# Attention weights turned in quarters of the array: 32 products of 64x64 in place of eight full transposes

## The chip, the core and the metric

The kernel runs on one core of one Trainium2 chip. The metric is the device time of one execution in microseconds. Work on a core is shared among TensorE (PE, matmuls, written to PSUM), VectorE (DVE), ScalarE (ACT), GpSimd (POOL, unused here but for set-up) and the DMA queues (SP issues them).

## What is computed

Attention within chunks of 64 tokens, and behind it a channel mix with a shift by one token. All tensors are FP32; 8 batches, 8 heads, 576 tokens, head size 64, so 512 channels; the inner width of the mix is 1024.

```python
scores = scale * np.matmul(q_c, k_c.transpose(0, 1, 2, 4, 3))   # chunks of 64 tokens
scores = scores - np.max(scores, axis=-1, keepdims=True)
attn = np.exp(scores)
attn = attn / (np.sum(attn, axis=-1, keepdims=True) + 1e-09)
x = np.matmul(attn, v_c)                                        # back to [batch, token, channel]
xk = mu_k * x + (1.0 - mu_k) * x_prev                           # x_prev: the token before
xr = mu_r * x + (1.0 - mu_r) * x_prev
k = np.maximum(xk @ w_k, 0.0)
out = 1.0 / (1.0 + np.exp(-(xr @ w_r))) * (k * k @ w_v)
```

## The kernel before

The 4608 tokens are cut into 18 groups of 256, each two tiles (`tl`) of 128 tokens, each of these two chunks of 64 (`e`). Groups 0 to 2 are done in an opening whose steps stand in a list of their own (`START`). From group 2 on `group(g)` records the steps of a group under names, and the table `GROUP` sets by hand in which order they are issued; no scheduler changes it (`manual_schedule`). While group g goes through the mix, the attention of group g + 1 is done between its products. `group_attention` is called with g + 1 for 15 groups, 3 to 17; these are the regular groups that the change touches.

Attention of a group runs like this. `group_products` (`s`, L973) multiplies queries and keys: 32 products of 64x64 by 64 columns, each in one quarter of the array. The rows of the array that a product uses follow from the partitions of its operands, the columns from the partitions of its output. VectorE and ScalarE make the weights `pg` of it: `[token in chunk pair, tl, head, 64 keys]`, 128 partitions. The weights must then be turned, so that keys lie on partitions. That is `f_tr` (step `Pq.0`): eight transposes of 128x128, one for each tile and pair of heads (`hp`), go to `pt` in PSUM, two banks. `f_pT` (`Pq.1`, ScalarE) copies `pt` to `pTg`. `f_pv` (`Pq.2`) multiplies by the values into `xps` (L1058), again 32 products of 64x64 by 64 columns in quarters.

On TensorE the transposes stand between the last `pk` product (`moe_k`, L593, the first product of the mix) and the first `pr` product (`moe_r`, L647, 24 of them). Behind `pr` come `xps`, the scores `s` of the group after, and the products `vx` and `vyz` (L870) of the mix. `pk`, `pr`, `vx` and `vyz` use the whole array, with operands in F32R; attention and its transposes are in F32. In the opening, `move_qk` (`trk` and `trq`, L357) turns queries and keys by plain matmuls with `ident`, 64 columns of the array at a time:

```python
for hp in range(HP):
    for j in range(2):
        nc.tensor.matmul(
            x[halves[j], hp, :],
            T[f"{nm}{g}"][:, j * HP + hp, r, :],
            ident,
```

Of the kernel before, what the change touches and what calls it, by code (L numbers as in the profile page):

```python
# [7 lines left out]
F32 = mybir.dt.float32  # L8
# [3 lines left out]
AF = mybir.ActivationFunctionType  # L12
# [4 lines left out]
P = 128  # L17
CH = 64
TT = 128
# [60 lines left out]
def tile_chunk_attention_channel_mix(  # L80
# [12 lines left out]
    nc = tc.nc  # L93
# [3 lines left out]
    HP = H // 2  # L97
# [23 lines left out]
    ps_s = ctx.enter_context(tc.tile_pool(name="ps_s", bufs=1, space=PSUM))  # L121
# [5 lines left out]
    T = {}  # L127
# [5 lines left out]
    ident = const.tile([P, P], F32, name="ident")  # L133
# [128 lines left out]
    def quarter(h, c):  # L262

        n = 10 * (h + 1) + c + 1
        if n not in B:
            B[n] = wts.tile([P, 2, HF, HD], F32R, tag=f"b{n}", name=f"b{n}")
        return B[n]
# [77 lines left out]
    halves = [slice(j * CH, (j + 1) * CH) for j in range(2)]  # L345
# [99 lines left out]
    def x_tile(g):  # L445
        return xp.tile([P, NB, G + 4], F32, tag="x", name=f"x_{g}")

    def x_cuts(t):

        cut = -t * TT % S  # L450
        if 0 < cut < TT:
            return [(0, cut, 0), (cut, TT - cut, cut + 1)]
        return [(0, TT, 0)]
# [533 lines left out]
    def group_attention(g):  # L987
        do.task = f"S{g}c"

        def heads(x):  # L990
            return x.rearrange("p t h c -> p (t h) c")

        def scores():
            return T[f"s{g}"].rearrange("p j t h c -> p j (t h) c")

        def p():
            return heads(T[f"pg{g}"])

        def f_max(_):
            m = T[f"m{g}"] = par_m.tile([P, 2, H], F32, tag="m", name=f"m_{g}", bufs=1)  # L1000
            nc.vector.tensor_reduce(out=m, in_=scores(), axis=AX.X, op=ALU.max)

        def f_sub(_):
            T[f"pg{g}"] = att.tile([P, 2, H, CH], F32, tag="p", name=f"p_{g}", bufs=1)
            m = T[f"m{g}"].unsqueeze(3).to_broadcast([P, 2, H, CH])
            to = T[f"pg{g}"].rearrange("p t (h j) c -> p j (t h) c", j=2)
            nc.vector.tensor_tensor(to, scores(), m, ALU.subtract)

        def f_exp(_):
            nc.scalar.activation(p(), p(), AF.Exp, scale=1.0 / D**0.5)  # L1010

        def f_z(_):
            T[f"z{g}"] = par_z.tile([P, 2 * H], F32, tag="z", name=f"z_{g}", bufs=1)
            nc.vector.tensor_reduce(out=T[f"z{g}"], in_=p(), axis=AX.X, op=ALU.add)

        def f_eps(_):
            nc.vector.tensor_scalar_add(T[f"z{g}"], T[f"z{g}"], 1e-9)

        def f_inv(_):
            nc.vector.reciprocal(T[f"z{g}"], T[f"z{g}"])  # L1020

        def f_norm(_):
            z = T[f"z{g}"].unsqueeze(2).to_broadcast([P, 2 * H, CH])
            nc.vector.tensor_tensor(p(), p(), z, ALU.mult)

        do(f_max, "D")
        do(f_sub, "D")
        do(f_exp, "A")
        do(f_z, "D")
        do(f_eps, "D")  # L1030
        do(f_inv, "D")
        do(f_norm, "D")

        do.task = f"P{g}q"

        def f_tr(_):
            T[f"pt{g}"] = ps_s.tile([P, 2, HP, TT], F32, tag="s", name=f"pt_{g}")
            for tl in range(2):
                for hp in range(HP):
                    nc.tensor.transpose(  # L1040
                        out=T[f"pt{g}"][:, tl, hp, :],
                        in_=T[f"pg{g}"][:, tl, 2 * hp : 2 * hp + 2, :],
                        identity=ident,
                    )

        def f_pT(_):
            T[f"pTg{g}"] = att.tile([P, 2, HP, TT], F32, tag="p", name=f"pT_{g}", bufs=1)
            nc.scalar.activation(T[f"pTg{g}"], T[f"pt{g}"], AF.Copy)

        def f_pv(_):  # L1050
            T[f"xps{g}"] = ps_x.tile([P, NB, G], F32, tag="x", name=f"xps_{g}")
            for tl in range(2):
                for a in range(HP // 2):
                    for e in range(2):
                        for c in range(2):
                            for j in range(2):
                                hp = 2 * a + c
                                nc.tensor.matmul(  # L1058
                                    T[f"xps{g}"][
                                        halves[c], 2 * j + a, tl * TT + e * CH : tl * TT + (e + 1) * CH  # L1060
                                    ],
                                    T[f"v{2 * g + tl}"][halves[j], hp, e, :],
                                    T[f"pTg{g}"][halves[j], tl, hp, halves[e]],
                                    start=True,
                                    stop=True,
                                )

        def f_open(_):
            x = T[f"xg{g}"] = x_tile(g)
            if g * G % S == 0:  # L1070
                nc.vector.memset(x[:, :, 0:1], 0.0)
            elif g == 3:
                seg = x_cuts(2 * g - 1)[-1]
                last = seg[2] + seg[1]
                nc.vector.tensor_copy(out=x[:, :, 0:1], in_=xt[2 * g - 1][:, :, last : last + 1])
            else:
                s, n, c = group_cuts(g - 1)[-1]
                nc.vector.tensor_copy(out=x[:, :, 0:1], in_=T[f"xg{g - 1}"][:, :, c + n : c + n + 1])
            for s, n, c in group_cuts(g)[1:]:
                nc.vector.memset(x[:, :, c : c + 1], 0.0)  # L1080

        def f_x(_):
            for s, n, c in group_cuts(g):
                nc.scalar.activation(
                    T[f"xg{g}"][:, :, c + 1 : c + 1 + n], T[f"xps{g}"][:, :, s : s + n], AF.Copy
                )

        do(f_tr, "P")
        do(f_pT, "A")
        do(f_pv, "P")  # L1090
        do(f_open, "D")
        do(f_x, "A")

    def group_cuts(g):
        cut = -g * G % S
        if 0 < cut < G:
            return [(0, cut, 0), (cut, G - cut, cut + 1)]
        return [(0, G, 0)]
# [52 lines left out]
    for i in range(4):  # L1151
        h = i // 2
# [5 lines left out]
            lambda s, h=h, part=part: [quarter(h, c)[:, s, part, :] for c in range(2)],  # L1158
            ("kk", "kk", "st", "st")[i],
        )  # L1160
    for t in range(6):
# [5 lines left out]
        if t in (1, 3):  # L1167
            g = t // 2
# [12 lines left out]
    with tc.manual_schedule():  # L1181
        for word in START.split():
            name, _, e = word.partition(":")
# [105 lines left out]
```

## Time and profile before

| | us |
|---|---|
| median of 3 runs | 562.09 |
| lowest and highest of them | 561.68, 562.21 |
| the profiled execution, its own time | 561.84 |
| its span, first to last instruction | 560.1 |
| TensorE busy | 553.5 (99%) |
| VectorE busy | 462.8 (83%) |
| ScalarE busy | 346.1 (62%) |
| matmuls recorded on TensorE | 6432 |

The table is read so: the span is the profiled execution's time less what lies around it (1.7 us here); an engine's busy time is the time in which at least one of its instructions ran. Matmuls overlap in the array, so one of 64 columns is shown with some 218 ns though the next starts long before that is over; their pace is read from starts, not from durations.

### The profile page before, as it was taken

The numbers are of one execution on the slowest core, as the hardware profiler recorded it, in microseconds if no ns is written. First come the engines' busy times: TensorE is split into PE (matmuls) and PEld (weight loads), VectorE is DVE, ScalarE is ACT, GpSimd is POOL, SyncE is SP. The second block draws the span as 40 slices with busy tenths as digits, with TensorE's granted clock in tenths as the row PEclk, the third lists the DMA queues.
The fourth block names the chain that finished last, engine by engine and source line by source line (L and its number), as shares of the span: only waits on it lengthen the run. The fifth ranks groups of instructions, "written<-read, shape, count | busy, mean of one in ns | idle before, by whom it ended". The sixth has DMA issues, their size and how long they took to land.

```text
span 560.1 us, 15245 instructions
## 1 busy us (share of the span) xinstructions
PE 553.5 (99%) x6432; PEld 526.1 (94%) x6432; DVE 462.8 (83%) x789; ACT 346.1 (62%) x509; POOL 0.7 (0%) x6
## 2 busy tenths in 40 slices
PE   9999999999999999999999999999999999999997
PEld 8888999999999999999999999999999999999997
DVE  2999999999897879787888978887888788876834
ACT  5899941739474756657565747483929292938461
POOL 0000000000000000000000000000000000000000
PEclk9999999999999999999999999999999999999999
DMA  9997534444343433421243434343343402010011
GB/s 284 278 285 204 133 76 94 69 69 110 67 107 66 94 69 79 69 72 40 57 67 94 66 89 66 91 71 90 65 99 59 103 1 76 3 45 33 3 38 37
DMA packets 184276, 49.24 MB, mean 88 GB/s; under 512 B 169608, under 2 KB 176272, under 8 KB 184208
## 3 DMA queue, kind: packets, MB, share of 16 engines
q1 hardware_dynamic: 183904, 48.01, 37.9%
q8 instruction: 50, 0.82, 0.7%
q10 hardware_dynamic: 304, 0.27, 0.1%
q14 instruction: 18, 0.15, 0.1%
HBM read 38.80 MB, written 9.44 MB: 86 GB/s over the span
## 4 chain that ended last, share of the span: by engine, by line
PE 90%; ACT 7%; DMA 2%; DVE 0%; issue 0%; ACTq 0%
PE pk L593 33%; PE pr L647 16%; PE vx L870 15%; PE vyz L870 11%; PE pv L681 6%; PE xps L1058 3%; PE s L973 3%; PE pt L1040 2%; DMA k_ring<-in_k 2%; PE warm L1186 1%; ACT wk L141 1%; PE trk L357 1%; ACT wv_st L295 1%; ACT wv_st L299 1%; ACT relu L614 0%; ACT wk_st L299 0%
## 5 line engine op out<-in xcount | busy, mean ns | idle before, releaser
L593 PE MATMUL pk<-xkhi,wk 128*128 128x256 f32 (+1 forms) x1167 | 202.0, 276 | 0.2 <-ACT relu L614 0.2
L593 PEld LDWEIGHTS pk<-xkhi,wk 128*128 128x128 f32 x1167 | 177.1, 188 | 0.7 <-ACT relu L614 0.4
L593 PE MATMUL pk<-xklo,wk 128*128 128x256 f32 x576 | 160.0, 278 | 0.1
L593 PEld LDWEIGHTS pk<-xklo,wk 128*128 128x128 f32 x576 | 108.2, 188 | 0.5 <-DVE xklo L566 0.5
L614 ACT ACTIVATE rr<-pk 128x512 f32<-128x512 f32 x60 | 35.3, 589 | 114.3 <-PE pk L593 114.3
L647 PE MATMUL pr<-wr,xrhi 128*128 128x512 f32 x288 | 90.4, 395 | 0.0
L870 PE MATMUL vx<-b,ks 128*128 128x256 f32 x540 | 68.5, 276 | 0.0
L870 PE MATMUL vyz<-b,kk 128*128 128x256 f32 x540 | 68.5, 276 | 0.0
L870 PEld LDWEIGHTS vyz<-b,kk 128*128 128x128 f32 x540 | 64.5, 188 | 0.0
L870 PEld LDWEIGHTS vx<-b,ks 128*128 128x128 f32 x540 | 64.5, 188 | 0.0
L647 PEld LDWEIGHTS pr<-wr,xrhi 128*128 128x128 f32 x288 | 52.7, 188 | 10.3
L647 PE MATMUL pr<-wr,xrlo 128*128 128x512 f32 x144 | 56.2, 390 | 0.0
L899 ACT ACTIVATE u<-vx 128x256 f32<-128x256 f32 x30 | 11.5, 384 | 54.3 <-PE vx L870 54.3
L708 DVE TENSOR_TENSOR kk<-rr,kk 128x1024 fp32r<-128x1024 f32 x30 | 35.4, 1222 | 10.7 <-ACT kk L854 10.6
L621 ACT ACTIVATE rr<-rr 128x512 f32<-128x512 f32 x60 | 38.0, 633 | 1.9
L708 DVE TENSOR_TENSOR xklo<-mk,xkhi 128x1024 fp32r<-128x1024 f32 x15 | 18.4, 1225 | 25.1 <-ACT xkhi L1130 25.1
L681 PE MATMUL pv<-b,kk 128*128 128x256 f32 (+1 forms) x290 | 34.3, 278 | 0.0
L681 PEld LDWEIGHTS pv<-b,kk 128*128 128x128 f32 x290 | 33.4, 188 | 0.1
L647 PEld LDWEIGHTS pr<-wr,xrlo 128*128 128x128 f32 x144 | 27.0, 188 | 5.7
L708 DVE TENSOR_TENSOR ks<-ss,ks 128x512 fp32r<-128x512 f32 x45 | 28.3, 684 | 0.0
L1120 DVE SCALAR_TENSOR_TENSOR mk<-d,mu,x 128x256 f32<-128x256 f32 (+3 forms) x80 | 27.7, 413 | 0.4
L1120 DVE SCALAR_TENSOR_TENSOR mr<-d,mu,x 128x256 f32<-128x256 f32 (+3 forms) x80 | 27.5, 411 | 0.0
(119 smaller groups left out, 839.4 us busy)
## 6 DMA issues: line engine op xcount, KB each, us to landing
v<-in_v SPq DMA_DIRECT2D x144, 64.0 KB, 2.6
out<-sg SPq DMA_DIRECT2D x34, 256.0 KB, 2.3
q_ring<-in_q SPq DMA_DIRECT2D x192, 36.0 KB, 2.1
k_ring<-in_k SPq DMA_DIRECT2D x192, 36.0 KB, 2.2
wk_st<-in_moe_w_k SPq DMA_DIRECT2D x4, 1024.0 KB, 9.4
wv_st<-in_moe_w_v SPq DMA_DIRECT2D x4, 1024.0 KB, 7.5
wr_st<-in_moe_w_r SPq DMA_DIRECT2D x2, 1024.0 KB, 8.1
k_ring<-in_k SPq DMA_DIRECT2D x2, 512.0 KB, 7.3
```

What stands on the lines that cost most here:

```text
L593: nc.tensor.matmul(pk[:, e, part], wk[a][:, cb, f * P : (f + 1) * P], xk[b][:, cb, part], start=(n == 0 and part is parts[0]), stop=(n == ...
L614: nc.scalar.activation(r, T[f"pk{g}{fp}"], AF.Relu)
L621: nc.scalar.activation(r, r, AF.Square)
L647: nc.tensor.matmul(pr, xr[a][:, cb, tl * TT : (tl + 1) * TT], wr[b][:, cb, :], start=(n == 0), stop=(n == 3 * NB - 1),)
L681: nc.tensor.matmul(T[f"pv{g}{tl}"][:, cols[c]][:, part], kk[a][:, f, tok[tl]], quarter(f // HF, c)[:, b, f % HF, part], start=(f == 0 and ...
L708: nc.vector.tensor_tensor(to, x, y, ALU.subtract)
L870: nc.tensor.matmul(to, a[i][:, f, :], weight(w, j, f), start=first and f == 0 and n == 0, stop=f == HF - 1 and n == 2, skip_group_check=True,)
L899: nc.scalar.activation(T[f"u{g}"][n // 2][:, n % 2], src(), AF.Copy)
L973: nc.tensor.matmul(T[f"s{g}"][halves[e], j, tl, hp, :], qT[halves[j], hp, cols], kT[halves[j], hp, cols], start=True, stop=True,)
L1040: nc.tensor.transpose(out=T[f"pt{g}"][:, tl, hp, :], in_=T[f"pg{g}"][:, tl, 2 * hp : 2 * hp + 2, :], identity=ident,)
L1058: nc.tensor.matmul(T[f"xps{g}"][halves[c], 2 * j + a, tl * TT + e * CH : tl * TT + (e + 1) * CH], T[f"v{2 * g + tl}"][halves[j], hp, e, :] ...
L1120: nc.vector.scalar_tensor_tensor(out=to[:, cb, s : s + w], in0=T[f"d{g}"][:, cb, s : s + w], scalar=mu[:, cb : cb + 1], in1=T[f"xg{g}"][:, ...
```

## The change

In `f_tr` each transpose of 128x128 gives way to four plain matmuls, one for each quarter: the moving operand is a 64x64 block of `ident`, the stationary one a 64x64 block of the weights (chunk `e`, head `2 * hp + j`). That is 32 products for a group. `pt` takes another layout, with `e` outside, so that the products of one half of the array's rows write one bank. `f_pT` copies the same 1024 elements of each partition and puts them in the old order as it writes, in runs of 64. `pTg` and all that reads it stay as they are, and so does the transposing in the opening (`att_values`).

```diff
--- before.py
+++ after.py
@@ -1034,18 +1034,26 @@
         do.task = f"P{g}q"
 
         def f_tr(_):
-            T[f"pt{g}"] = ps_s.tile([P, 2, HP, TT], F32, tag="s", name=f"pt_{g}")
+            T[f"pt{g}"] = ps_s.tile([P, 2, 2, HP, CH], F32, tag="s", name=f"pt_{g}")
             for tl in range(2):
                 for hp in range(HP):
-                    nc.tensor.transpose(
-                        out=T[f"pt{g}"][:, tl, hp, :],
-                        in_=T[f"pg{g}"][:, tl, 2 * hp : 2 * hp + 2, :],
-                        identity=ident,
-                    )
+                    for e in range(2):
+                        for j in range(2):
+                            nc.tensor.matmul(
+                                T[f"pt{g}"][halves[j], e, tl, hp, :],
+                                T[f"pg{g}"][halves[e], tl, 2 * hp + j, :],
+                                ident[halves[e], halves[e]],
+                                start=True,
+                                stop=True,
+                            )
 
         def f_pT(_):
             T[f"pTg{g}"] = att.tile([P, 2, HP, TT], F32, tag="p", name=f"pT_{g}", bufs=1)
-            nc.scalar.activation(T[f"pTg{g}"], T[f"pt{g}"], AF.Copy)
+            nc.scalar.activation(
+                T[f"pTg{g}"].rearrange("p t h (e c) -> p e (t h) c", e=2),
+                T[f"pt{g}"].rearrange("p e t h c -> p e (t h) c"),
+                AF.Copy,
+            )
 
         def f_pv(_):
             T[f"xps{g}"] = ps_x.tile([P, NB, G], F32, tag="x", name=f"xps_{g}")
```

No step changes its place. TensorE's instructions around the turn in one of the regular groups, from the last two `pk` products to the third `pr`, are these before (in a row: line, operation, output and operands, size of the output, count):

```order
L593 MATMUL pk_3_3258<-xklo_3035,wk_118 128x256
L593 MATMUL pk_3_3258<-xkhi_3034,wk_119 128x256
L1040 MATMUL pt_3283<-ident,p_3175 128x128 x8
L647 MATMUL pr_0_3313<-wr_120,xrhi_3180 128x512
L647 MATMUL pr_0_3313<-wr_121,xrhi_3180 128x512
L647 MATMUL pr_0_3313<-wr_120,xrlo_3181 128x512
```

and these with the change:

```order
L593 MATMUL pk_3_3354<-xklo_3131,wk_118 128x256
L593 MATMUL pk_3_3354<-xkhi_3130,wk_119 128x256
L1042 MATMUL pt_3379<-ident,p_3271 64x64 x32
L647 MATMUL pr_0_3433<-wr_120,xrhi_3276 128x512
L647 MATMUL pr_0_3433<-wr_121,xrhi_3276 128x512
L647 MATMUL pr_0_3433<-wr_120,xrlo_3277 128x512
```

Only the row in the middle is another one: 32 matmuls of 64x64 stand where eight of 128x128 stood, behind the same `pk` and ahead of the same `pr`.

## Rows read from the trace of the kernel before

**Rows 1.** The page: busy time, share and instructions; TensorE's granted clock by slices.
```profile
PE 553.5 (99%) x6432; PEld 526.1 (94%) x6432; DVE 462.8 (83%) x789; ACT 346.1 (62%) x509; POOL 0.7 (0%) x6
...
PEclk9999999999999999999999999999999999999999
```

**Rows 2.** The page's chain that ended last, by line.
```profile
PE pk L593 33%; PE pr L647 16%; PE vx L870 15%; PE vyz L870 11%; PE pv L681 6%; PE xps L1058 3%; PE s L973 3%; PE pt L1040 2%; DMA k_ring<-in_k 2%; PE warm L1186 1%; ACT wk L141 1%; PE trk L357 1%; ACT wv_st L295 1%; ACT wv_st L299 1%; ACT relu L614 0%; ACT wk_st L299 0%
```

**Rows 3.** The chain in order of time, a regular group: start us, us, what.
```profile
444.38 11.01 PE pk L593 x97
455.38 0.87 PE pt L1040 x8
456.26 5.47 PE pr L647 x24
461.73 1.09 PE xps L1058 x64
462.82 0.93 PE s L973 x64
463.75 1.57 PE vx L870 x12
465.32 1.36 PE vyz L870 x12
```

**Rows 4.** Line L1040, whole span: records, min/median/max ns; what TensorE waited for.
```profile
L1040 PE MATMUL pt<-ident,p x120: 270/272/273, 104.3 to 514.2; 128*128 128x128 f32 x120
its engine sat idle before it (us, times) until:
```

**Rows 5.** Timeline of TensorE around one `pt`: start us, us, instructions.
```profile
455.10 0.28 PE L593 MATMUL pk<-xkhi,wk 128*128 128x256 f32 x1
455.22 1.03 PE L1040 MATMUL pt<-ident,p 128*128 128x128 f32 x8
...
456.56 0.40 PE L647 MATMUL pr<-wr,xrlo 128*128 128x512 f32 x1
```

**Rows 6.** Timeline of TensorE in the last group.
```profile
541.49 0.28 PE L593 MATMUL pk<-xkhi,wk 128*128 128x256 f32 x1
...
542.07 0.39 PE L647 MATMUL pr<-wr,xrlo 128*128 128x512 f32 x1
```

**Rows 7.** Lines L973 and L357, whole span (x: records; ns).
```profile
L973 PE MATMUL s<-kT,qT x960: 218/218/267, 92.2 to 492.6; 64*64 64x64 f32 x192
...
L357 PE MATMUL trk<-ident,k_ring x96: 272/273/475, 5.3 to 30.6; 128*64 128x128 f32 x96
```

**Rows 8.** Timeline of TensorE from `pr` to `xps` and `s`.
```profile
461.34 0.39 PE L647 MATMUL pr<-wr,xrlo 128*128 128x512 f32 x1
461.66 1.16 PE L1058 MATMUL xps<-pT,v 64*64 64x64 f32 x64
462.64 1.11 PE L973 MATMUL s<-kT,qT 64*64 64x64 f32 x64
```

**Rows 9.** Timeline of TensorE in the opening: products in quarters, then `pr`.
```profile
24.08 0.69 PE L400 MATMUL s<-kT,qT 64*64 64x64 f32 x32
24.59 0.65 PE L484 MATMUL xps<-pT,v 64*64 64x64 f32 x32
...
25.74 0.40 PE L647 MATMUL pr<-wr,xrlo 128*128 128x512 f32 x1
```

**Rows 10.** Timeline of TensorE from `pv` to `s`.
```profile
122.51 0.50 PE L681 MATMUL pv<-b,kk 128*128 128x256 f32 x3
122.94 0.28 PE L973 MATMUL s<-kT,qT 64*64 64x64 f32 x3
```

**Rows 11.** Timelines of VectorE and of ScalarE around the same `pt`.
```profile
452.74 1.23 DVE L1024 TENSOR_TENSOR p<-p,z 128x1024 f32<-128x1024 f32 x1
...
456.59 1.01 ACT L1048 ACTIVATE pT<-pt 128x1024 f32<-128x1024 f32 x1
```

**Rows 12.** Timeline of TensorE at L357 in the opening.
```profile
15.66 0.61 PE L357 MATMUL trk<-ident,k_ring 128*64 128x128 f32 x8
```

## Prediction

> **What bounds the kernel now.** I began with the page's busy shares [rows 1]: TensorE is busy for 553.5 of 560.1 us and its granted clock reads 9 (0.9 or more of full speed) in all 40 slices; VectorE has 83% and ScalarE 62%. A high busy share alone doesn't say that every nanosecond of an engine counts, so the chain that ended last came next [rows 2]: its large shares all belong to TensorE, and the changed line L1040 is on it with 2%. In order of time [rows 3] a regular group is TensorE and nothing else, piece on piece: `pk`, `pt` (0.87 us), `pr`, `xps`, `s`, then seven pieces of `vx` and `vyz`. Last I looked at the changed line itself [rows 4]: 120 transposes, eight in each of 15 groups, and nothing is listed under what TensorE sat idle for ahead of them. So what the change adds to TensorE's time here, or takes from it, should go into the span in full, 15 times.
>
> **What is taken away.** The price of the eight transposes is read between two fixed points: the start of the last `pk` product and the start of the third `pr` product (the first on `xrlo`, which has a row of its own). With the transposes between them that is 456.56 - 455.10 = 1.46 us [rows 5]; in the last group, which has none, 542.07 - 541.49 = 0.58 us [rows 6]. So the eight cost 0.88 us, 0.11 us each, and hardly anything at the edges.
>
> **What is put in its place.** Each group gets 32 products of 64x64 by 64 columns, in the four quarters of the array. The kernel already has this very shape, 32 at a time: `s` at L973 (2x4x2x2 turns of the loops) and `xps` at L1058. What decides is how much work one such product is. The rows say two: 960 matmuls are recorded at L973 for 15 x 32 = 480 products [rows 7], and `xps` and `s` have 64 records in a group [rows 8], while a `transpose` at L1040 leaves one, 120 for 120 [rows 4]. The records that double are those of plain products of two F32 operands. That it is not a matter of quarters shows at L357, which also multiplies by `ident` with a plain matmul: 2x3 steps of 8 products turn the keys, 48, and 96 records stand for them [rows 7]. The new lines are written as L357 is, so I count 64 records, not 32.
>
> Their pace: `xps` starts at 461.66 and the `s` behind it at 462.64 [rows 8], 0.98 us for 64 records; `s` itself, which comes from quarters, has 0.93 in the chain [rows 3], 0.058 us for four records, one in each quarter. The same work followed by `pr` stands in the opening: 32 records of `s` and 32 of `xps` start at 24.08, and the third `pr` starts at 25.74 [rows 9], 1.66 us with all that the return to the whole array costs. Missing is the way in. From the last `pr` to the first `xps` 461.66 - 461.34 = 0.32 us pass [rows 8], where `pr` products follow each other in 5.47/24 = 0.23 [rows 3], 0.09 more; behind `pk` products, 11.01/97 = 0.11 apart [rows 3], that makes 0.20. (From `pv` to `s` it is the same: three `pv` start at 122.51 and end 0.50 later; one lasts 0.28 as `pk` does, so the last starts at 122.73, and `s` at 122.94 [rows 5, 10].) Sum: 0.20 + 1.66 = 1.86 us from the last `pk` to the third `pr` against 1.46, so **+0.41 us a group** (0.409 with unrounded starts). Of that the 64 records are 0.93, the changes of the array's division in and out 0.36, and 0.88 are saved.
>
> The Trainium skill (TensorE: Matmul & The Clock Gate, section Terms) says that the transpose mode of trn2 is four times faster for FP32. The rows agree that a plain F32 product costs more than a transpose, but at two records, not four times. By the page's factor a plain 128x128 product would take 4x0.11 us, one of half as many columns 0.22, and eight rounds of four in quarters 1.74 us instead of 0.93, +12 us more over the kernel, 580 us in all; the 64 records of `xps` in 0.98 us [rows 8] speak against it, and nothing in the sum uses it.
>
> **What else moves.** The copy `pT` on ScalarE reads the same 1024 elements but writes them in runs of 64. It takes 1.01 us now and ends at 457.60 [rows 11], and `xps`, which reads it, starts at 461.66 [rows 8] behind 24 `pr` products: 4.06 us of cover, in which even a copy of twice the time would be hidden. So I take nothing for it; without cover a second 1.01 us would be 15 us. VectorE's normalised `p` ends at 453.97, 1.25 us before `pt` starts [rows 5, 11], so the wait at the head of the new products is met as before. The memory of `pt` and the order of the steps don't change, so no DMA and no queue moves. All that stands behind `pt` comes later together, which gives VectorE and ScalarE more room, not less. I see no wait on TensorE that could swallow the 0.41 us.
>
> The total: 15 x 0.409 = +6.1 us. The profiled execution took 561.84 us, which gives 568.0; the median of the runs is 562.09, 0.25 above it, so on that footing the forecast is 568.2 us (+1.1%).
>
> **Rivals.**
> A, not slower: the products leave one record each, as the transposes do. Then eight rounds of 0.058 us fall away, 0.47 us, and a group is 0.06 us shorter: 15 x 0.06 = 0.9, 561.2 us. It decides at 36 records in a block: 0.41 us are seven rounds of four, 28 records fewer than 64. Against it stand the doubled records of L357, L973 and L1058. 0.05.
> B, much slower: the new order puts two products on the same half of the rows, one behind the other (`e` is outside, `j` inside), where `s` and `xps` change the half of the rows with each. If two of one half can't run at once, a round of four takes twice 0.058: 15 x 16 x 0.058 = +14 us more, 582 us. Against it: at L357 all products share all rows and go to alternate halves of the columns, and eight records start within 0.61 - 0.27 = 0.34 us [rows 7, 12], three rounds of two and a bit, 0.11 us a round; one whole-array transpose alone takes that. Two on the same rows do overlap there. 0.07. The Trainium skill has a rule in this direction (same page, Part 3, what overlaps): a weight load overlaps matmuls in flight only where the row group differs. It would give this rival's time; the L357 rows, where weights load for the same rows throughout, speak against it. The factor of four above would end near this time too, and has its share of this chance.
> C, about the same: the way in and out is cheaper than at the places that I read. With nothing for it, a group is 0.93 - 0.88 = 0.05 us longer, 562.9 us. Against it: the way in costs alike behind `pr` and behind `pv`, and after every `s` the first piece of `vx` takes 1.57 us where the pieces behind it take 1.36 [rows 3]. 0.03 for the whole of it, 0.05 for a part.
>
> **How the numbers follow.** The forecast has 0.80. Its own spread is small, since each term is a row of the same kernel at the same clock: 0.03 us a group in pace or edges is 0.5 us, and a part of C takes off up to 1.7 us. Range 566.5 to 571: a part of C below, a weak form of B above; it leaves out A, the whole of C, and B. About 0.2% (1.1 us) is what a measurement of this kernel can tell from no change. Slower: the forecast, B and the part of C, 0.92; same: A (0.16% faster) and the whole of C, 0.07; faster 0.01, for A with cheap edges.
>
> **What would show it.** In the profile after, the new line should have 960 matmuls of 64x64; 15 pieces of some 1.1 us in the chain where 0.87 stood; 0.20 us from the last `pk` to the first `pt`; the third `pr` 1.86 us behind the last `pk`; `xps`, `s` and all else as long as before, and no idle time ahead of `pr` and `xps`. 480 records would be A, a block of 1.9 us or more B. I would be wrong in kind if TensorE waited somewhere for what the trace doesn't show, for then the 0.41 us would vanish there.

## Result and profile after

The changed kernel takes 569.12 us (median of 4 runs, 569.08 to 569.44), the kernel before 562.15 (561.68 to 562.44 in the runs beside it): a ratio of 1.0126 with a 95% interval of 1.0108 to 1.0144, slower by 7.0 us (6.1 to 8.1 by the interval). The forecast was 568.2 us, range 566.5 to 571.

The page of the changed kernel, its span, busy times, TensorE's granted clock and the chain that ended last, answers to [rows 1] and [rows 2]:

```profile
span 567.3 us, 16925 instructions
...
PE 559.8 (99%) x7272; PEld 529.3 (93%) x7272; DVE 463.0 (82%) x789; ACT 347.6 (61%) x509; POOL 0.7 (0%) x6
...
PEclk9999999999999999999999999999999999999999
...
PE 92%; SPq 3%; ACT 2%; DMA 2%; issue 0%; DVE 0%; ACTq 0%
PE pk L593 34%; PE pr L647 17%; PE vx L870 15%; PE vyz L870 11%; PE pv L681 6%; PE xps L1066 3%; PE pt L1042 3%; PE s L973 3%; DMA k_ring<-in_k 2%; SPq L199 2%; SPq L291 1%; SPq L184 1%; ACT wk L141 1%; ACT wk_st L299 0%; ACT wk_st L295 0%; PE xps L484 0%
```

TensorE is still busy in 99% of a longer span, at the same clock, and 840 more matmuls are recorded (7272 for 6432): 960 have come and 120 are gone. VectorE's busy time has hardly moved (463.0 us for 462.8). The chain's rows of SP, which issues the DMA, all stand in the opening, before 19 us. The new line by itself, and what TensorE waited for ahead of it (the view of [rows 4]):

```profile
L1042 PEld LDWEIGHTS pt<-ident,p x960: 129/135/135, 104.9 to 520.9; 64*64 64x64 f32 x192
L1042 PE MATMUL pt<-ident,p x960: 218/218/267, 104.9 to 520.9; 64*64 64x64 f32 x192
its engine sat idle before it (us, times) until:
```

32 products in 15 groups left 960 records, two each, every one with a weight load, and again no idle time is listed. The timeline of TensorE around one turn, start and length in us (the view of [rows 5], the group shown there):

```profile
460.70 0.28 PE L593 MATMUL pk<-xkhi,wk 128*128 128x256 f32 x1
460.91 1.16 PE L1042 MATMUL pt<-ident,p 64*64 64x64 f32 x64
462.00 0.72 PE L647 MATMUL pr<-wr,xrhi 128*128 128x512 f32 x2
462.56 0.40 PE L647 MATMUL pr<-wr,xrlo 128*128 128x512 f32 x1
```

From the last `pk` product to the first `pt` 0.21 us pass, and from it to the third `pr` 462.56 - 460.70 = 1.86 us, where 1.46 stood before. The chain through the same group (the view of [rows 3]):

```profile
449.98 11.00 PE pk L593 x97
460.98 1.09 PE pt L1042 x64
462.07 5.68 PE pr L647 x24
467.75 1.09 PE xps L1066 x64
468.84 0.93 PE s L973 x64
469.78 1.57 PE vx L870 x12
471.35 1.36 PE vyz L870 x12
...
479.51 10.55 PE pk L593 x93
```

The `pt` piece is 1.09 us instead of 0.87 and the `pr` piece behind it 5.68 instead of 5.47; `pk`, `xps`, `s`, `vx` and `vyz` are as they were. From one `pk` piece to the next it is 479.51 - 449.98 = 29.53 us; in the kernel before, where the `pk` piece behind that of [rows 3] is

```profile
473.48 11.01 PE pk L593 x97
```

it is 473.48 - 444.38 = 29.10. The copy `pT` (the view of [rows 11] by line; min/median/max ns) takes no more in runs of 64 than in one:

```profile
L1052 ACT ACTIVATE pT<-pt x15: 1006/1007/1012, 106.2 to 521.2; 128x1024 f32<-128x1024 f32 x15
```

### The profile page after: what moved, and what is told of

Its sections match the earlier page's. It is cut to its first block, busy times and chain, and to the rows that moved or that the text cites. A ratio compares the mean times of both kernels' runs of the same rounds, so it can differ in the third digit from the quotient of the medians.

```text
span 567.3 us, 16925 instructions
## 1 busy us (share of the span) xinstructions
PE 559.8 (99%) x7272; PEld 529.3 (93%) x7272; DVE 463.0 (82%) x789; ACT 347.6 (61%) x509; POOL 0.7 (0%) x6
## 4 chain that ended last, share of the span: by engine, by line
PE 92%; SPq 3%; ACT 2%; DMA 2%; issue 0%; DVE 0%; ACTq 0%
PE pk L593 34%; PE pr L647 17%; PE vx L870 15%; PE vyz L870 11%; PE pv L681 6%; PE xps L1066 3%; PE pt L1042 3%; PE s L973 3%; DMA k_ring<-in_k 2%; SPq L199 2%; SPq L291 1%; SPq L184 1%; ACT wk L141 1%; ACT wk_st L299 0%; ACT wk_st L295 0%; PE xps L484 0%
```

## Experiments

Theory 1 is that of the prediction: a plain F32 product is two records of work where a transpose is one, four records (one in each quarter) take 0.058 us, and the division of the array (whole, in halves or in quarters) is changed once in and once out, which has a price of its own. The others are named in the expectations. Each run has the kernel before beside it on the same chip; its medians there were 562.65 (e2 to e5; 15 runs, 561.47 to 563.63) and 562.27 us (e1, e6; 15 runs, 561.68 to 562.99). Where rounding shifts the difference of two starts, that of the unrounded starts is given too; it is the same to a few ns in all 15 groups.

**e1_plain_full: plain products without quarters.** An edit of the kernel before, `pt` and `pT` as there:

```diff
-                    nc.tensor.transpose(
-                        out=T[f"pt{g}"][:, tl, hp, :],
-                        in_=T[f"pg{g}"][:, tl, 2 * hp : 2 * hp + 2, :],
-                        identity=ident,
+                    nc.tensor.matmul(
+                        T[f"pt{g}"][:, tl, hp, :],
+                        T[f"pg{g}"][:, tl, 2 * hp : 2 * hp + 2, :],
+                        ident,
+                        start=True,
+                        stop=True,
```

> The kernel before, its eight transposes of 128x128 written as eight plain F32 products with ident, whole array, no quarters. Theory 1 (a plain F32 product is two records of work, a transpose one): 240 matmuls on the line instead of 120, 16 records of 0.11 us a group, 0.88 us a group more than before and no changes of the division, 15 x 0.9 = 13.4 us, 575.5 us (574 to 577). Theory 4 (a whole-array product with ident costs what the transpose costs, and the doubling belongs to the quarters): the time of the kernel before, 562.

Measured: 575.86 us, ratio 1.0246 (1.0232 to 1.0260). The line's records, and the timeline of TensorE around one turn:

```profile
L1040 PE MATMUL pt<-ident,p x240: 270/275/275, 104.9 to 528.1; 128*128 128x128 f32 x120
```

```profile
136.35 0.28 PE L593 MATMUL pk<-xkhi,wk 128*128 128x256 f32 x1
136.47 1.95 PE L1040 MATMUL pt<-ident,p 128*128 128x128 f32 x16
...
138.71 0.39 PE L647 MATMUL pr<-wr,xrlo 128*128 128x512 f32 x1
```

120 products left 240 records, and the third `pr` stands 138.71 - 136.35 = 2.36 us behind the last `pk`, 0.90 more than with transposes (0.91 unrounded); 15 x 0.91 = 13.6 us, and 13.6 were measured. The array is never divided at this place. So the doubling belongs to the plain F32 product and not to the quarters, and theory 4 is out.

**e2_alternate: the order of the quarters.** An edit of the changed kernel:

```diff
-                    for e in range(2):
-                        for j in range(2):
+                    for j in range(2):
+                        for e in range(2):
```

> The loops over e and j are exchanged, so that the half of the array's rows changes with each product, as in s and xps. Theory 1 (a plain product is two records, and the array's division is changed once in and once out): the order costs nothing, 1.86 to 1.88 us from the last pk to the third pr, the time of the changed kernel, 569.1 us within 0.5. Theory 2 (two products on the same half of the rows get in each other's way, and that is the part of the loss that the sum missed): the block gets shorter and the kernel faster by 0.5 us or more.

Measured: 568.94 us, ratio 1.0112 (1.0097 to 1.0128), where the changed kernel has 1.0126 (1.0108 to 1.0144). Timeline of TensorE around the same turn:

```profile
460.33 0.28 PE L593 MATMUL pk<-xkhi,wk 128*128 128x256 f32 x1
460.54 1.16 PE L1042 MATMUL pt<-ident,p 64*64 64x64 f32 x64
...
462.19 0.40 PE L647 MATMUL pr<-wr,xrlo 128*128 128x512 f32 x1
```

1.86 us from `pk` to the third `pr`, as with the other order. Two products of this shape in turn on the same half of the rows don't get in each other's way; theory 2, the rival B of the prediction in any form, is out.

**e3_whole_between: two more changes of the division.** An edit of the changed kernel:

```diff
             for tl in range(2):
+                if tl == 1:
+                    nc.tensor.transpose(
+                        out=T[f"pt{g}"][:, 0, 1, 0:2, :],
+                        in_=T[f"pg{g}"][:, 1, 0:2, :],
+                        identity=ident,
+                    )
                 for hp in range(HP):
```

> Between the 16 products of the first tile and the 16 of the second one whole-array transpose is put in (its output is overwritten by the products behind it), so the division changes twice more per group. Theory 1: 0.11 us for the transpose and some 0.36 for the two changes, 0.47 us a group, 15 x 0.47 = 7.0 us over the changed kernel, 576 us (574.5 to 577.5). Theory 3 (the loss lies in the number of records alone, and changes of the division cost nothing of note): 0.11 us a group, 1.7 us, 570.8.

Measured: 575.03 us, ratio 1.0223 (1.0207 to 1.0239), 5.9 us over the changed kernel and 6.1 over e2, which ran beside it. Timeline of TensorE around one turn:

```profile
105.89 0.28 PE L593 MATMUL pk<-xkhi,wk 128*128 128x256 f32 x1
106.10 0.69 PE L1048 MATMUL pt<-ident,p 64*64 64x64 f32 x32
106.72 0.33 PE L1040 MATMUL pt<-ident,p 128*128 128x128 f32 x1
106.98 0.69 PE L1048 MATMUL pt<-ident,p 64*64 64x64 f32 x32
107.60 0.73 PE L647 MATMUL pr<-wr,xrhi 128*128 128x512 f32 x2
108.17 0.39 PE L647 MATMUL pr<-wr,xrlo 128*128 128x512 f32 x1
```

`pk` to the third `pr` is 108.17 - 105.89 = 2.28 us, 0.42 more than without the transpose, for 0.11 us of work. The changes of the division cost time and theory 3 is out; the pair of changes around this transpose cost 0.31 us, less than the 0.36 expected. (That the products behind it overwrite its output is not what costs: in e5 nothing is overwritten, and the price is the same.)

**e5_half: half of the products.** An edit of the changed kernel: the second tile goes back to whole transposes, which share the two banks of `pt` with the quarters of the first.

```diff
-            for tl in range(2):
-                for hp in range(HP):
-                    for e in range(2):
-                        for j in range(2):
-                            nc.tensor.matmul(
+            for hp in range(HP):
+                for e in range(2):
+                    for j in range(2):
+                        nc.tensor.matmul(
...
+            for hp in range(HP):
+                nc.tensor.transpose(
+                    out=wholes()[:, hp // 2, hp % 2, :],
+                    in_=T[f"pg{g}"][:, 1, 2 * hp : 2 * hp + 2, :],
+                    identity=ident,
+                )
```

> Only the first tile's weights are turned in quarters (16 products), the second tile's by four whole transposes; the copy pT is two instructions. Theory 1: 32 records are 0.47 us, the change in and out 0.36 to 0.38, saved are 4 x 0.11 = 0.44, so 0.40 us a group and +6.0 us over the kernel before, 568.1: half of the products cost as much as all of them. Theory 3 (loss in proportion to the products): half of 7.0, +3.5 us, 565.6.

Measured: 567.57 us, ratio 1.0085 (1.0071 to 1.0098), 4.9 us over the kernel before beside it: between the two figures, 6.0 and 3.5. The timeline says why:

```profile
104.83 0.28 PE L593 MATMUL pk<-xkhi,wk 128*128 128x256 f32 x1
105.03 0.69 PE L1047 MATMUL pt<-ident,p 64*64 64x64 f32 x32
105.66 0.66 PE L1055 MATMUL pt<-ident,p 128*128 128x128 f32 x4
106.07 0.71 PE L647 MATMUL pr<-wr,xrhi 128*128 128x512 f32 x2
106.61 0.39 PE L647 MATMUL pr<-wr,xrlo 128*128 128x512 f32 x1
```

`pk` to the third `pr` is 106.61 - 104.83 = 1.78 us, 0.32 more than before (0.34 unrounded), and 15 x 0.34 = 5.1. 32 records (0.47) for four transposes (0.44) account for 0.03 of it, the other 0.31 are the way in and out. So half of the products bring seven tenths of the loss: a fixed part is there, but it is 0.31 us where a transpose of 128 columns stands behind the quarters (here and in e3), not the 0.36 that were read where a `pr` of 512 columns does. Transposes and `pr` differ in type as well as in columns; which of the two sets the price was not tried.

**e4_row_halves: one record each, two at a time.** An edit of the changed kernel, whose layout and copy `pT` stay:

```diff
-                        for j in range(2):
-                            nc.tensor.matmul(
-                                T[f"pt{g}"][halves[j], e, tl, hp, :],
-                                T[f"pg{g}"][halves[e], tl, 2 * hp + j, :],
-                                ident[halves[e], halves[e]],
-                                start=True,
-                                stop=True,
-                            )
+                        nc.tensor.transpose(
+                            out=T[f"pt{g}"][:, e, tl, hp, :],
+                            in_=T[f"pg{g}"][halves[e], tl, 2 * hp : 2 * hp + 2, :],
+                            identity=ident[halves[e], halves[e]],
+                        )
```

> The changed kernel's layout, but turned by 16 transposes of 64 rows by 128 columns in two halves of the array's rows, which should leave one record each as the whole transposes do. Theory 1: eight rounds of two at 0.058 us are 0.47, the changes of the division 0.36 to 0.38, saved are 0.88, so 0.04 us a group less than before, 561.4 us (560.8 to 562.2). Theory 2: transposes in two halves of the rows do not run at once, 16 x 0.058 = 0.93 us, and the time is that of the changed kernel, 569.

Measured: 561.88 us against 562.65, ratio 0.9987 (0.9978 to 0.9996): faster than both kernels, by 0.13%, hardly more than can be told. The line, and the timeline around one turn:

```profile
L1041 PEld LDWEIGHTS pt<-ident,p x240: 135/138/140, 105.0 to 514.0; 64*128 64x128 f32 x120
L1041 PE MATMUL pt<-ident,p x240: 222/223/272, 105.0 to 514.1; 64*128 64x64 f32 x120
```

```profile
455.24 0.28 PE L593 MATMUL pk<-xkhi,wk 128*128 128x256 f32 x1
455.45 0.71 PE L1041 MATMUL pt<-ident,p 64*128 64x64 f32 x16
456.09 0.73 PE L647 MATMUL pr<-wr,xrhi 128*128 128x512 f32 x2
456.65 0.39 PE L647 MATMUL pr<-wr,xrlo 128*128 128x512 f32 x1
```

16 transposes in a group, 240 records. `pk` to the third `pr` is 456.65 - 455.24 = 1.41 us, 0.05 less than with whole transposes (0.04 unrounded), and from `pt` to `pr` 0.64 us instead of 0.79. Theory 2 is out: 16 transposes one after the other would have taken 0.93. The changes of the division take back nearly all of what is won by two at a time. The rival A of the prediction would have looked like this: one record each, and a block slightly shorter.

**e6_f32r: one record in the whole array at the faster rate.** The weights are written in F32R (FP32 rounded to fewer digits, the type of the mix's operands), so that differences, exponentials and weights lose digits against the reference's FP32; `ident` is one F32R tile, read as F32 elsewhere.

```diff
-            T[f"pg{g}"] = att.tile([P, 2, H, CH], F32, tag="p", name=f"p_{g}", bufs=1)
+            T[f"pg{g}"] = att.tile([P, 2, H, CH], F32R, tag="p", name=f"p_{g}", bufs=1)
...
-                    nc.tensor.transpose(
+                    nc.tensor.matmul(
...
-                        identity=ident,
+                        ident_r,
+                        start=True,
+                        stop=True,
```

> As the kernel before, but the attention weights are written in F32R (differences, exponentials and weights are rounded to it, which gives up digits of the reference's FP32) and turned by eight plain whole-array products in F32R with ident in F32R. Theory 1 with pk's rows beside it (an F32R product is one record, a column takes half of what it takes in F32: 0.11 us for 256 columns of pk as for 128 of the transpose): 8 x 0.06 = 0.48 us a group instead of 0.88, 0.40 less and no changes of the division, 15 x 0.40 = 6.0 us less than before, 556.3 us (555.5 to 558). Rival: 128 columns a product are too few and the weight load bounds it at 0.11 us, then the time of the kernel before, 562.

Measured: 562.57 us, ratio 1.0004 (0.9995 to 1.0013), no change. Matmuls around one turn, and the weight loads of it:

```profile
251.52 0.28 PE L598 MATMUL pk<-xkhi,wk 128*128 128x256 f32 x1
251.63 1.00 PE L1048 MATMUL pt<-ident,p 128*128 128x128 f32 x8
...
253.00 0.39 PE L652 MATMUL pr<-wr,xrlo 128*128 128x512 f32 x1
```

```profile
251.52 0.97 PEld L1048 LDWEIGHTS pt<-ident,p 128*128 128x128 f32 x8
```

The eight products have one record each, yet `pk` to the third `pr` is 1.48 us, 0.02 more than before. Eight weight loads take 0.97 us with the last one's 0.19, 0.11 us apart. That the products themselves need as long is ruled out by the second of them, which starts 0.06 us behind the first (251.69 for 251.63):

```profile
251.69 0.39 PE L1048 MATMUL pt<-ident,p 128*128 128x128 f32 x2
```

The six behind it follow 0.11 us apart, each some 0.06 us behind the start of its own load. So the time is the rival's, and the starts bear out its reason: a product of 128 columns can follow in 0.06 us, but the loads come 0.11 us apart, and the faster rate for the columns that are moved brings nothing. What sets the spacing of the loads was not tried.

## Why the prediction came out

The steps held one by one. Two records for a plain product: 960 on the new line, and 240 for 120 in e1, where nothing is divided. The pace of the quarters, 0.058 us for four: the `pt` piece in the chain is 1.09 us, as long as the `xps` piece. The way in, 0.20 expected: 0.21. The block from `pk` to the third `pr`, 1.86 expected: 1.86. No wait on TensorE swallowed it (from 93 us to the end its view of waits is empty), and no work on ScalarE or VectorE took its place. A, B and C fell, A by the count of records, B by e2, C by e3 and the 1.86 us themselves.

The Trainium skill's rule on weight loads (TensorE: Matmul & The Clock Gate, Part 3, what overlaps), by which the order of the quarters would have mattered, is not borne out: both orders give 1.86 us. The Trainium skill's four times for the transpose mode (same page, Terms) are two here, by count of records and by e1: 0.88 us of transposes became 0.88 + 0.91.

What was short is the total, 6.1 us for 7.0. By the times alone that is hardly clear of noise: the interval begins at 6.1, and e2, with the same block, came out 568.94 - 562.65 = 6.3 us over the kernel before. Between the two profiled executions (spans 567.3 - 560.1 = 7.2) the difference can be followed. Three terms lie outside the block that I summed.
- The `pr` products behind the third: between that one and the first `xps` 5.12 us pass in the changed kernel (467.68 - 462.56) and 5.10 before, 0.016 unrounded, 15 x 0.016 = 0.2 us.
- The opening. The chain reaches the `s` ahead of the first turn at 92.80 us in the changed kernel, at 92.32 in the one before, and at 92.42 in e2, which runs the same opening. The changed kernel, then e2, in the chain:

```profile
92.80 1.09 PE s L973 x64
93.89 11.08 PE pk L593 x96
104.97 1.09 PE pt L1042 x64
```

```profile
92.42 1.09 PE s L973 x64
93.51 11.08 PE pk L593 x96
```

 No changed line has run by then, so 0.48 us of the two profiles' difference stood there already; openings of the six experiments differ by more than that (the same `s` at 92.41 to 93.99 us). The delay is there at the first `trk` behind the DMA of `k_ring`, 29.46 us for 28.95. Whether it varies from run to run or belongs to the program of each kernel isn't shown, since each left one profile.
- The last group. Its `vx` and `vyz` pieces take 1.41 us in the changed kernel, 1.36 in the one before, 0.3 to 0.4 us over seven of them:

```profile
548.65 5.46 PE pr L647 x24
554.11 1.41 PE vx L870 x12
555.52 1.41 PE vyz L870 x12
```

 That is so in e2 and e3 as well, which also turn both tiles in quarters, and not in e1, e4, e5 and e6. No line there was changed, and what sets it I didn't find out; it stays open.

With 15 x 0.41, 0.2, 0.5 and 0.35 the 7.2 us of the spans are accounted for. The step to mend is the one that summed only between `pk` and the third `pr` and took all else as equal: right for the groups to 0.02 us, but half a microsecond of the difference between two profiles stood there ahead of the first changed line. And the price of the division, 0.36 us, fitted because it was read with `pr` behind the quarters, as here; with transposes behind them it is 0.31 (e3, e5).

## What to carry to other kernels

Count what an operation leaves in the trace before pricing it: 32 quarter products look like half the work of eight transposes, a quarter of 32 x 64 columns for 8 x 128, until the records show that the plain F32 product counts twice. Then the quarters have nothing left to win (0.93 us for 0.88), and the change of the division, 0.31 to 0.36 us here, is all loss. Where packing does win, as in e4, the block has to be long enough to pay for that change, or to stand beside another block with the same division, as `s` does behind `xps`. Where TensorE is the bound and never idle, the measured price of a block between two fixed neighbours, times the number of blocks, gave the change to within 0.2 us in all six experiments, against 15 runs of the kernel before each, and to within 0.9 for the changed kernel, against four.

## What the runs showed of the hardware

- A plain F32 product with `ident` costs two records of 0.11 us at 128 columns, the `transpose` one (e1). In F32R it is one record, and still 0.11 us, the spacing of the weight loads, though a single one followed in 0.06 (e6).
- Transposes of 64 rows by 128 columns do run two at a time: 16 of them in 0.64 us, edges included (e4). Their loads have 128 columns too, and two such loads come in 0.06 us (from the first of a pair to the first of the next), where loads of 128x128 in e6 come 0.11 us apart. Those are loads of plain products, these of transposes, so the halves alone needn't be the reason.
- What a change of the division costs hangs on what follows: 0.36 us with `pr` products of 512 columns behind it, 0.31 with transposes of 128 (e3, e5).
